# Earlier issue of the first w_in quarter, held-back loads of the next group, and a new spacing of the first stages, in a fused attention and FFN kernel

## The chip, the cores and the metric

The kernel runs on one core of one Trainium2 chip. The metric is the device time of one execution in microseconds (us), lower is better. Executions of one kernel agree within about 1% here. All times below are medians of runs whose state is "fast" (or of a single profile, where that is said). Engines: PE (matrix), PEld (its weight loads), DVE (vector), ACT (scalar), POOL (GpSimd), SP (sync, which issues most DMA transfers). The program holds one list of instructions for each engine, and the framework puts semaphore waits in where one engine needs another's result.

## The reference

Sliding-window causal attention on q, k, v of shape (8, 8, 576, 64) with a window of 64 keys, then a feed-forward block on the 4608 tokens:

```python
scores = q @ k^T / sqrt(64);  only keys with 0 <= i - j < 64 count
attn   = softmax(scores) @ v            # -> x, 4608 x 512
h      = maximum(x @ w_in, 0)           # w_in 512 x 2048
out    = (h * h) @ w_out                # w_out 2048 x 512, result float32
```

## The kernel before

The 4608 tokens are 36 chunks of 128, taken in groups of four. Per chunk `S(i)` computes scores and the masked exponentials, `V(i)` multiplies them with v, `X(i)` transposes x, and `U(i, fq)` multiplies with one quarter of w_in; `TR` transposes k and q of a group; `out_proj`, the multiplication with w_out, follows a group later. Only the first two groups (the start) matter here; from group 2 on a steady loop runs.

v is kept in eight slots, each as two tiles: `v_ev[i]` holds chunk i, and `v_od[i]` holds the same rows shifted by 64, so that its lower half is the end of the chunk before. The cast of chunk i therefore writes three tiles, the last of them in the slot of its successor:

```python
    NV = 8
    def cast_v(i, st):
        v_ev, v_od, v_next = v_evs[i % NV], v_ods[i % NV], v_ods[(i + 1) % NV]
        nc.gpsimd.tensor_copy(out=v_ev[:, :, 0:D], in_=st[:])
        nc.gpsimd.tensor_copy(out=v_od[64:P, :, 0:D], in_=v_ev[0:64, :, 0:D])
        if i + 1 < NCK:
            nc.gpsimd.tensor_copy(out=v_next[0:64, :, 0:D], in_=v_ev[64:P, :, 0:D])
    # values(i), the value matmuls, read v_ods[i % NV] and v_evs[i % NV], all 128 rows
```

The start of the program, in order of emission (cut):

```python
    nc.vector.memset(v_ods[0][0:64, :, 0:D], 0.0)
    ...                                  # casts and transposes of k, q of group 0
    for i in range(2):
        cast_v(i, vst[i])                # POOL
    for quar in range(3):
        load_w_in(quar)                  # POOL issues: float32 in HBM, float16 in SBUF
    for i in range(2, 4):
        cast_v(i, vst[i])
    kst[1], qst[1] = load_kq(k, 1), load_kq(q, 1)   # SP issues
    for i in range(4, 8):
        vst[i] = load(v, i)
    ...                                  # casts of k, q of group 1, load_w_in(3)
    warm(2), S(0), warm(2), S(1), warm(3)
    V(0), S(2), warm(2), X(0), V(1), S(3), X(1), warm(1), V(2), U(0, 0), X(2), V(3), U(1, 0)
    ...
    U(3, 2), TR("q", 1, 0, acopy)
    for i in range(4, 8):
        cast_v(i, vst[i])
        if i > 4:
            load_w_out(i - 5)
    load_w_out(3)
    U(0, 3), ...
```

The program is emitted by one Python thread. The framework works out semaphore waits from the order of emission: a read waits for the writes of the same bytes that were emitted ahead of it, and a write for the reads emitted ahead of it. `warm` is a matmul on zeros that is meant to keep the clock up.

The softmax here doesn't subtract the row's maximum and nothing guards it: scores larger than these inputs give would overflow.

## Time and profile before

| what | value | view |
|---|---|---|
| median time of the first three runs | 337.8 us | runs |
| PE busy | 92% of 337.3 us | page, part 1 |
| longest wait of PE | 7.1 us, for w_in | waits |
| mean granted clock, 20 to 40 us | 0.74 | windows |
| first matmul of group 2's `up` | 99.5 us | timeline |

From the page: the span in 40 slices of 8.4 us, each digit the busy share in tenths (PEclk: the granted clock in tenths).

```profile
PE   7728987799899999999999999999999999999994
PEclk9976997799999999999999999999999999999999
DMA  7999999942929569958989796989589021100111
```

The loss is in the first eight slices or so: PE has gaps, the clock falls, and DMA is busy all the time. After that PE is full.

Waits of PE in the first 120 us (engine, line, what for, us in total, times, longest):

```profile
PE hps L293 <- DMA w_in<-in_moe_w_in_dram: 7.1, 1, 7.1
PE xt_ps L257 <- DVE x_sb L247: 5.0, 7, 2.2
...
```

The timeline of PE (start, duration, what; in brackets the idle time before it and its releaser) shows the wait and the cold clock: the first `U`, 16 matmuls, takes 1.89 us, and 1.06 us when warm.

```profile
14.57 0.22 PE L242 MATMUL av<-v_od,pm 128*64 128x65 f16 x1
...
26.87 1.89 PE L293 MATMUL hps<-xT,w_in 128*128 128x128 f16 x16 [7.15 <-DMA w_in<-in_moe_w_in_dram]
...
44.43 1.06 PE L293 MATMUL hps<-xT,w_in 128*128 128x128 f16 x16
```

The DMA view of two windows of 1 us, from 20 and from 21 us (queue: packets, MB, share of the 16 DMA engines). q0 carries the transfers that POOL issues, q1 those of SP. w_in, issued at 14.59, moves nothing before 21.4 us:

```profile
q1 hardware_dynamic: 148, 0.15, 109.0%
...
q1 hardware_dynamic: 182, 0.19, 69.9%
q0 software_dynamic: 64, 0.07, 38.6%
```

### The profile page before, as it was taken

How to read it: one execution, taken by the hardware profiler on the slowest of the kernel's cores; microseconds unless marked ns; L12 is line 12 of the kernel's file. 1: busy time of each engine (PE TensorE's matmuls, PEld its weight loads, DVE VectorE, ACT ScalarE, POOL GpSimd, SP SyncE). 2: the span in 40 equal slices, each digit the busy share in tenths (PEclk: the TensorE clock that was granted, in tenths of full speed). 3: DMA queues.
4: the chain of work that ended last, by engine and by line, in shares of the span. 5: the costliest groups of instructions: out<-in, count | busy, mean ns of one | idle time of the engine just before them, and what ended most of it. 6: DMA issues, size and time to landing. Idle time of an engine off the chain costs nothing.

```text
span 337.3 us, 7237 instructions
## 1 busy us (share of the span) xinstructions
PE 308.7 (92%) x2891; PEld 165.8 (49%) x2891; DVE 183.5 (54%) x424; ACT 158.6 (47%) x272; POOL 113.4 (34%) x188
## 2 busy tenths in 40 slices
PE   7728987799899999999999999999999999999994
PEld 3317976578444544454444444444443444444441
DVE  3753676554666664575476557646574665334400
ACT  3612693237445554553555355545544554444311
POOL 1782682780526160535063416333451000000000
PEclk9976997799999999999999999999999999999999
DMA  7999999942929569958989796989589021100111
GB/s 248 206 221 200 221 220 198 219 86 73 180 87 194 121 134 225 211 119 191 226 154 206 151 230 123 212 171 231 119 186 216 35 62 32 63 31 33 62 62 63
DMA packets 136737, 50.79 MB, mean 151 GB/s; under 512 B 121856, under 2 KB 132096, under 8 KB 136704
## 3 DMA queue, kind: packets, MB, share of 16 engines
q1 hardware_dynamic: 132480, 46.15, 65.2%
q0 software_dynamic: 4224, 4.19, 7.3%
q8 instruction: 22, 0.36, 0.5%
q14 instruction: 11, 0.09, 0.1%
HBM read 36.70 MB, written 9.44 MB: 137 GB/s over the span
## 4 chain that ended last, share of the span: by engine, by line
PE 59%; DMA 19%; DVE 7%; ACT 6%; SPq 5%; POOL 2%; issue 2%; POOLq 0%; ACTq 0%
PE ops L310 26%; PE hps L281 19%; DMA qT<-q 7%; PE hps L293 7%; DMA st<-in_v_dram 7%; DMA w_in<-in_moe_w_in_dram 4%; PE av L242 3%; PE sc L218 3%; DVE h L275 3%; ACT hrelu L274 2%; SPq L196 2%; DVE pm L231 2%; ACT pm L227 1%; DVE x_sb L247 1%; ACT qT L191 1%
## 5 line engine op out<-in xcount | busy, mean ns | idle before, releaser
L275 DVE SCALAR_TENSOR_TENSOR h<-hps,hrelu 128x512 f16<-128x512 f32 x144 | 99.4, 690 | 119.6 <-ACT hrelu L274 119.1
L310 PE MATMUL ops<-w_out,h 128*128 128x512 f16 x576 | 146.5, 381 | 0.0
L274 ACT ACTIVATE hrelu<-hps 128x512 f32<-128x512 f32 x144 | 86.2, 599 | 116.7 <-PE hps L281 81.6
L281 PE MATMUL hps<-xT,w_in 128*128 128x512 f16 x448 | 115.1, 379 | 0.0
L310 PEld LDWEIGHTS <-h 128*128 128x128 f16 x576 | 53.8, 98 | 60.5 <-issue 0.5
L281 PEld LDWEIGHTS <-w_in 128*128 128x128 f16 x448 | 42.8, 98 | 50.1
L227 ACT ACTIVATE pm<-sc 128x512 f16<-128x512 f32 x72 | 39.0, 597 | 22.4 <-PE sc L218 21.8
L293 PE MATMUL hps<-xT,w_in 128*128 128x128 f16 x512 | 36.6, 233 | 8.4 <-DMA w_in<-in_moe_w_in_dram 7.1
L113 POOL CAST k<-st 128x512 f16<-128x512 f32 x24 | 14.9, 620 | 83.4 <-DMA st<-in_k_dram 71.9
L293 PEld LDWEIGHTS <-w_in 128*128 128x128 f16 x512 | 33.4, 105 | 11.2 <-DMA w_in<-in_moe_w_in_dram 7.3
L125 POOL CAST v_ev<-st 128x512 f16<-128x512 f32 x36 | 22.6, 629 | 35.3 <-DMA st<-in_v_dram 28.5
L316 ACT ACTIVATE osb<-ops 128x512 f32<-128x512 f32 x36 | 21.6, 599 | 22.8 <-PE ops L310 22.7
L247 DVE TENSOR_TENSOR x_sb<-av,rden 128x256 f16<-128x256 f32 x72 | 30.5, 424 | 2.5
L231 DVE TENSOR_TENSOR pm<-pm,mask_inner 128x512 f16<-128x512 f16 x56 | 26.6, 499 | 4.5 <-ACT pm L227 4.1
L126 POOL COPY v_od<-v_ev 64x512 f16<-64x512 f16 x36 | 22.5, 624 | 2.3
L128 POOL COPY v_od<-v_ev 64x512 f16<-64x512 f16 x35 | 22.2, 634 | 2.0
L242 PEld LDWEIGHTS <-pm 128*64 128x64 f16 x576 | 12.8, 113 | 15.6 <-issue 9.5
L242 PE MATMUL av<-v_od,pm 128*64 128x65 f16 x288 | 17.4, 200 | 1.7 <-DVE pm L231 1.6
L113 POOL CAST q<-st 128x512 f16<-128x512 f32 x24 | 14.8, 618 | 9.7 <-DMA st<-in_q_dram 9.7
L242 PE MATMUL av<-v_ev,pm 128*64 128x65 f16 x288 | 17.4, 201 | 0.0
L218 PE MATMUL sc<-qT,kT 64*128 64x64 f16 x504 | 15.0, 191 | 0.5 <-ACT qT L179 0.3
L218 PEld LDWEIGHTS <-kT 64*128 64x128 f16 x504 | 10.7, 95 | 4.1 <-issue 2.7
(56 smaller groups left out, 118.2 us busy)
## 6 DMA issues: line engine op xcount, KB each, us to landing
out_dram<-osb SPq DMA_DIRECT2D x36, 256.0 KB, 2.6
st<-in_v_dram SPq DMA_DIRECT2D x32, 256.0 KB, 5.8
st<-in_k_dram SPq DMA_DIRECT2D x21, 256.0 KB, 4.3
st<-in_q_dram SPq DMA_DIRECT2D x21, 256.0 KB, 4.9
w_in<-in_moe_w_in_dram POOLq DMA_DIRECT2D x4, 512.0 KB, 14.4
w_out<-in_moe_w_out_dram POOLq DMA_DIRECT2D x4, 512.0 KB, 13.0
kq_st<-in_k_dram SPq DMA_DIRECT2D x1, 1024.0 KB, 5.5
kq_st<-in_q_dram SPq DMA_DIRECT2D x1, 1024.0 KB, 8.0
```

The lines of the kernel that those rows point to most:

```text
L113: copy(out=kq16(key, i // 4)[:, :, i % 4, :].rearrange("p a (b d) -> p a b d", d=D), in_=st[:].rearrange("p (a b) d -> p a b d", b=2))
L125: nc.gpsimd.tensor_copy(out=v_ev[:, :, 0:D], in_=st[:])
L218: nc.tensor.matmul(sc[hh][:, hp, blk, :], keys, qTs["q", g][r0:r0 + 64, hp, a + 64 * blk:a + 64 * blk + 64], start=True, stop=True)
L227: nc.scalar.activation(out=pm[:], in_=sc[hh][:], func=AF.Exp, scale=1.0 / float(D) ** 0.5)
L231: nc.vector.tensor_tensor(out=pm[:], in0=pm[:], in1=mask, op=ALU.min)
L242: nc.tensor.matmul(av[64 * blk:64 * blk + 64, h % 4, 0:65], pms[i][h % 2][:, h // 2, blk, :], vv[:, h, 0:65], start=True, stop=True)
L247: nc.vector.tensor_tensor(out=x_sb[:, 2 * half:2 * half + 2, i % 2, :].rearrange("p c (b d) -> p c b d", d=D), in0=av[:, :, 0:D].rearrange ...
L274: nc.scalar.activation(out=hrelu, in_=hps, func=AF.Relu, scale=H_SCALE)
L275: nc.vector.scalar_tensor_tensor(out=out, in0=hps, scalar=0.0, in1=hrelu, op0=ALU.max, op1=ALU.mult)
L281: nc.tensor.matmul(hps[:], w_in_q[f // 4][:, c, f % 4 * P:(f % 4 + 1) * P], xT_of(g)[:, :, c, :], start=(c == 0), stop=(c == DMC - 1))
L293: nc.tensor.matmul(hps[:, f, :], w_in_q[fq][:, c, f * P:(f + 1) * P], xT_of(g)[:, i % 4 // 2, c, a:a + P], start=(c == 0), stop=(c == DMC ...
L310: nc.tensor.matmul(hold[ts % 2][:], h2s["h", g][:, 4 * fq + f, ts * P:(ts + 1) * P], w_out_q[fq][:, f, :], start=(fq == 0 and f == 0), sto ...
```

## The change

The intent: bring the first w_in quarter in earlier. It is issued behind the cast of chunk 0 instead of chunk 1; the loads of the next group are held back by a 2-byte transfer that reads the second w_in quarter, so that SP issues nothing more until that quarter has landed; the same is done with w_out and group 2. The first stages are then spaced anew, and the casts of v chunks 4 to 7 are written further up in the program. The core of the diff:

```diff
+    gate16 = const.tile([1, 8], FP16, name="gate16")
+    def behind(w, n):
+        nc.sync.dma_start(out=gate16[:, n:n + 1], in_=w[0:1, 0, 0:1])
@@ start
-    for i in range(2):
-        cast_v(i, vst[i])
-    for quar in range(3):
-        load_w_in(quar)
+    cast_v(0, vst[0])
+    load_w_in(0)
+    cast_v(1, vst[1])
+    load_w_in(1)
+    load_w_in(2)
     for i in range(2, 4):
         cast_v(i, vst[i])
+    behind(w_in_q[1], 0)
     kst[1], qst[1] = load_kq(k, 1), load_kq(q, 1)
@@ the same loop, moved up over the first S, V, X, U
+    for i in range(4, 8):
+        cast_v(i, vst[i])
+        if i > 4:
+            load_w_out(i - 5)
+    load_w_out(3)
     warm(2), S(0), warm(2), S(1), warm(3)
-    V(0), S(2), warm(2), X(0), V(1), S(3), X(1), warm(1), V(2), U(0, 0), X(2), V(3), U(1, 0)
+    V(0), S(2), warm(3), V(1), X(0), S(3), warm(2), V(2), X(1), U(0, 0), V(3), X(2), U(1, 0)
     ... (U, TR, S of group 0 and 1 reordered, six more warm matmuls)
-    for i in range(4, 8):
-        cast_v(i, vst[i])
-        if i > 4:
-            load_w_out(i - 5)
-    load_w_out(3)
+    behind(w_out_q[1], 1)
     kst[2], qst[2] = load_kq(k, 2), load_kq(q, 2)
@@ spacing of group 1: new fractions, e.g.
-        steps += [(0.01 + 0.08 * j, V, 4 + j), (0.05 + 0.08 * j, X, 4 + j)]
+        steps += [(0.02 + 0.1 * j, V, 4 + j)] if j else []
+        steps += [(0.03 + 0.115 * j, X, 4 + j)]
     ...
-                steps.append((0.88, transposes_xbar, g + 2))
+                steps.append((0.8, transposes_xbar, g + 2))
```

## The prediction

> **What bounds it.** Over the whole span PE is 92% busy, and from 140 us on it is bound by PE (58.6 of 60 us busy, windows view). The loss lies in the first 70 us, which DMA bounds: the 40 slices show DMA at 90% or more there and 2 tenths just after 70.
>
> - PE waits 7.15 us (19.6 to 26.9, timeline) for the first w_in quarter. It was issued at 14.59 and landed 12.2 us later. The DMA queues by 1 us window show no byte of the software queue before 21.3 us; until then the hardware queue moved group 1's k and q. The first w_out quarter did the same: issued at 40.2, first bytes 46.6.
> - The idle time drops the granted clock to 0.50 from 22 to 32 us; an up_chunk takes 1.9 us there, against 0.9 warm: about 2.9 us lost.
> - From 50 to 66 us come waits on x_sb and xT (2.2, 0.7, 1.6 us) and two more cold stretches (0.5 to 0.6): about 8 us in all.
>
> Total loss before 100 us: 18 to 20 us.
>
> **Why w_in is late.** The Trainium skill ("DMA: Bandwidth & Descriptors", "Queues, rings and completion order") says that an engine round-robins between queues at packet granularity. The trace agrees once both flow (about 155 packets of each per us, 27 to 34 us), not for the 6 us before. My reading: descriptors of the hardware queue already taken in (some 1,100 packets, 70 per engine) go first. Rival: a software DMA has some 6 us of latency anyway. No view separates them; I give the first 75%.
>
> **The change.** Engine orders differ only before group 2: SP gains two 2-byte transfers and keeps its order, POOL moves one w_in issue up by one cast_v (2.0 us), PE reorders and gains six warm matmuls (0.2 us each). From group 2 on all orders are equal; moving transposes_xbar from 0.88 to 0.80 passes nothing on SP, so it is worth 0.
>
> **Expected course.** First w_in issue 12.6 instead of 14.6, bytes from about 14.3 (v finishes at 13.7), a quarter takes 3.1 to 3.4 us of packets: landing about 18, before U(0,0) needs it (19.3). The 7 us wait and the cold stretch go: about 9 us ahead at U(0,1). Given back: group 1's k and q now start at about 22 instead of 13.5 and land at about 27.5 and 32; the fourth w_in, issued behind the cast of k, lands about 36, so U(0,3) waits 1 to 2 us. V(4) comes about 7 us earlier than 48.4. Then w_out flows without competition at about 40, kq of group 2 starts near 48 behind the second w_out, and the wider spacing should take some 3 to 5 us of the x_sb and cold losses. Some waits for late TR and v_8 casts come back.
>
> Sum: 9 − 2 + 4 − 1 = about 10 us, nearly all on the critical path, since all after it is PE-bound and unchanged.
>
> **Predicted:** 327.5 us (range 320.5 to 336.5). Faster by over 2%: 0.74; within 2%: 0.23; slower: 0.03.
>
> **What would show it.** Right: first software-queue bytes at 14 to 15 us; no wait of U for w_in above 1 us; granted clock 1.00 from 20 to 32 us; the first L281 matmul of group 2 near 89 instead of 99.6; equal periods (32 us) after. Wrong: bytes at about 19 (issue + 6) mean the latency theory; then w_in costs 3.5 us still and the fourth quarter lands at 44 to 46, with a wait of 5 us or more before U(0,3), and the gain shrinks to 0 to 3 us.
>
> **What would make it wrong.** That latency; kq of group 2 landing after 60 us and stalling TR; DVE (about 70% busy once the stage is squeezed) becoming the limit.

## More of the kernel before

POOL, same view: the three w_in issues, and the last copy of `cast_v(7)`, the one that writes `v_ods[0]`.

```profile
14.59 2.36 POOL L138 DMA_DIRECT2D w_in<-in_moe_w_in_dram  x3
...
44.99 0.61 POOL L128 COPY v_od<-v_ev 64x512 f16<-64x512 f16 x1
```

So `V(0)` ran at 14.57, thirty microseconds ahead of that copy.

## The result, and the profile after

| kernel | median us (runs) | ratio to before, 95% interval |
|---|---|---|
| before | 337.99 (337.05 to 339.36) | |
| changed | 360.25 (359.33 to 360.89) | 1.0653 (1.0606 to 1.0700) |

The result is correct, and 6.5% slower. All ratios in this document are the mean time of one kernel's fast runs over the mean of the other's fast runs of the same rounds, so they are not quite the ratio of the medians quoted.

The page of the changed kernel (span 357.3 us, slices of 8.9 us):

```profile
PE   8400098879999999999999999999999999999994
PEclk9955569989999999999999999999999999999999
DMA  7999899970018759695799879599967611300021
```

PE does nothing at all for three slices. The waits of PE, in a window from 10 to 115 us:

```profile
PE av L247 <- POOL v_od L129: 30.7, 1, 30.7
PE xt_ps L262 <- DVE x_sb L252: 2.7, 5, 1.7
PE hps L298 <- DVE xT L265: 1.5, 2, 1.2
...
```

The wait for w_in is gone. In its place stands one single wait of 30.7 us, of the value matmuls (L247) for a v_od copy of POOL. The timelines of PE and of POOL name both ends of it:

```profile
13.90 0.82 PE L307 MATMUL warm<-zeros 128*128 128x512 f16 x3
45.44 0.22 PE L247 MATMUL av<-v_od,pm 128*64 128x65 f16 x1 [30.72 <-POOL v_od L129]
```
```profile
12.56 0.87 POOL L139 DMA_DIRECT2D w_in<-in_moe_w_in_dram  x1
...
44.78 0.61 POOL L129 COPY v_od<-v_ev 64x512 f16<-64x512 f16 x1
```

The copy that ends at 45.39 is the last one of `cast_v(7)`; `V(0)` starts 0.05 us after it. What `V(0)` waits for is not its own v, cast by 12.6 us, but the v of chunk 7.

The DMA side did what was predicted. In the changed kernel the 1 us windows from 13 and from 14 us give:

```profile
q1 hardware_dynamic: 174, 0.04, 26.5%
...
q0 software_dynamic: 47, 0.05, 50.9%
```

The first w_in bytes move at 14.1 us, 7.3 us earlier than before. And the stages behind the stall are shorter: `V(0)` is 30.9 us later than before (45.44 against 14.57), but group 2's first `up` matmul only 20.5 us later (119.9 against 99.5), and the span 20.0 us longer. That is no sign that the cure works: e2 below has the stall but neither the early w_in nor the new spacing, and its stages are shortened as much (first value matmul at 44.96 us, group 2 at 119.9). The loads land while PE stands still (in e2 all four w_in quarters by 36.8 us). Under the stall the rest of the change is worth 1 us at most (360.25 against 361.23 us in e2), which is within the scatter.

**Theory A.** `V(0)` is now emitted behind `cast_v(7)`, which writes the lower half of `v_ods[0]`. The framework has to take this as a read after a write, and makes `V(0)` wait for chunk 7's cast. In the kernel before it was a write after a read, which POOL had long to satisfy. **Rival B:** the held-back loads make the v chunks late, and `V(0)` shows it. **Rival C:** the emission of the loop ahead of the matmuls costs as such, whatever the slot.

### The profile page after: what moved, and what is told of

Its sections match the earlier page's. It is cut to its first block, busy times and chain, and to the rows that moved or that the text cites. A ratio compares the mean times of both kernels' runs of the same rounds, so it can differ in the third digit from the quotient of the medians.

```text
span 357.3 us, 7251 instructions
## 1 busy us (share of the span) xinstructions
PE 308.1 (86%) x2897; PEld 164.7 (46%) x2897; DVE 185.1 (52%) x424; ACT 158.9 (44%) x272; POOL 113.0 (32%) x188
## 4 chain that ended last, share of the span: by engine, by line
PE 53%; DMA 20%; POOL 7%; SPq 6%; DVE 6%; ACT 5%; issue 2%; POOLq 0%; ACTq 0%
PE ops L315 23%; PE hps L286 17%; DMA st<-in_v_dram 7%; DMA qT<-q 7%; PE hps L298 6%; PE sc L223 3%; PE av L247 3%; DMA kq_st<-in_q_dram 3%; DVE h L280 3%; SPq L201 2%; ACT hrelu L279 2%; SPq L84 2%; POOL v_ev L126 2%; POOL v_od L127 2%; DMA w_in<-in_moe_w_in_dram 2%
## 5 line engine op out<-in xcount | busy, mean ns | idle before, releaser
L286 PEld LDWEIGHTS <-w_in 128*128 128x128 f16 x448 | 42.8, 98 | 50.1
L247 PE MATMUL av<-v_od,pm 128*64 128x65 f16 x288 | 17.0, 201 | 31.6 <-POOL v_od L129 30.7
L298 PE MATMUL hps<-xT,w_in 128*128 128x128 f16 x512 | 33.6, 224 | 2.0 <-DVE xT L265 1.5
L247 PEld LDWEIGHTS <-pm 128*64 128x64 f16 x576 | 12.9, 114 | 46.0 <-issue 40.2
L298 PEld LDWEIGHTS <-w_in 128*128 128x128 f16 x512 | 31.0, 100 | 4.8 <-issue 2.9
L321 ACT ACTIVATE osb<-ops 128x512 f32<-128x512 f32 x36 | 21.6, 600 | 24.4 <-PE ops L315 24.4
L251 DVE RECIPROCAL rden<-av 128x4 f32<-128x4 f32 x72 | 12.5, 173 | 30.5 <-PE av L247 30.4
L247 PE MATMUL av<-v_ev,pm 128*64 128x65 f16 x288 | 17.0, 202 | 0.0
```

What stands on the lines that cost most here:

```text
L247: nc.tensor.matmul(av[64 * blk:64 * blk + 64, h % 4, 0:65], pms[i][h % 2][:, h // 2, blk, :], vv[:, h, 0:65], start=True, stop=True)
L286: nc.tensor.matmul(hps[:], w_in_q[f // 4][:, c, f % 4 * P:(f % 4 + 1) * P], xT_of(g)[:, :, c, :], start=(c == 0), stop=(c == DMC - 1))
L298: nc.tensor.matmul(hps[:, f, :], w_in_q[fq][:, c, f * P:(f + 1) * P], xT_of(g)[:, i % 4 // 2, c, a:a + P], start=(c == 0), stop=(c == DMC ...
```

## The experiments

Ten kernels ran, one of them twice (e4 and e11); all gave correct results. "Before" ran in the same rounds on the same chip.

| run | what | us | ratio to before (95%) |
|---|---|---|---|
| e1_v0_first | changed, `V(0)` emitted ahead of the casts | 331.99 | 0.9801 (0.9761 to 0.9841) |
| e2_before_early | before, casts emitted early | 361.23 | 1.0672 (1.0637 to 1.0707) |
| e3_no_gates | changed, no held loads | 358.55 | 1.0585 (1.0546 to 1.0625) |
| e4_nine_slots | changed, nine v slots | 330.03 | 0.9745 (0.9712 to 0.9778) |
| e5_first_gate | e1, second hold removed | 330.33 | 0.9759 (0.9734 to 0.9784) |
| e6_no_gates_v0 | e1, both holds removed | 334.44 | 0.9882 (0.9855 to 0.9909) |
| e7_loads_only | before, early w_in and both holds | 336.94 | 0.9954 (0.9929 to 0.9978) |
| e8_spacing_only | e1, w_in as before, no holds | 335.00 | 0.9890 (0.9869 to 0.9911) |
| e9_nine_first_gate | e4, second hold removed | 330.50 | 0.9766 (0.9742 to 0.9789) |
| e10_fourth_early | e9, fourth w_in quarter earlier | 331.30 | 0.9796 (0.9769 to 0.9822) |
| e11_nine_again | e4 again | 330.30 | 0.9759 (0.9726 to 0.9793) |

### What makes the stall: e1 to e4

**e1_v0_first.** The edit moves `V(0)` over the loop, and with it the calls ahead of `V(0)`: the scores of chunks 0 and 1 and some warm matmuls, which had all run by 14.7 us in the changed kernel too. In the traces the instruction lists of all five engines are the same as in the changed kernel, instruction by instruction; only waits differ.

```diff
+    warm(2), S(0), warm(2), S(1), warm(3)
+    V(0)
     for i in range(4, 8):
         cast_v(i, vst[i])
         ...
-    warm(2), S(0), warm(2), S(1), warm(3)
-    V(0), S(2), warm(3), V(1), ...
+    S(2), warm(3), V(1), ...
```

> Only V(0), the value matmuls of chunk 0, is emitted ahead of the loop that casts v chunks 4 to 7; the order of instructions on each of the five engines is the same as in the changed kernel. Theory A (V(0) emitted behind cast_v(7) has to wait for it, because cast_v(7) writes the lower half of v_od slot 0, which V(0) reads): the 30.7 us wait of PE for v_od goes to under 1 us, the 357.3 us span falls to 322 to 330 us. Rival B (the held loads of group 1 make v late, so the wait stays): wait above 20 us, time within 5 us of the changed kernel's 360.

Measured 331.99 us, span 329.5, at the edge of what theory A gave for the span. The value matmuls start at 14.74 us; no wait for v_od is left among the waits of PE, whose longest in total are:

```profile
PE xt_ps L262 <- DVE x_sb L252: 2.1, 5, 1.2
PE av L247 <- DVE pm L236: 1.7, 4, 0.5
PE hps L298 <- DMA w_in<-in_moe_w_in_dram: 1.5, 1, 1.5
...
```

Rival B is refuted: the loads are held back exactly as in the changed kernel.

**e2_before_early.** The converse: the kernel before, with nothing but the loop of casts moved up. Here too all engines' lists are unchanged.

```diff
+    for i in range(4, 8):
+        cast_v(i, vst[i])
+        ...                  # w_out issues, as in the loop
     warm(2), S(0), warm(2), S(1), warm(3)
     V(0), ...
-    (the same loop, further down)
```

> The kernel before, with only the loop of casts of v chunks 4 to 7 (and w_out issues) emitted ahead of the first scores and V(0); engine orders unchanged, no held loads, old spacing. Theory A: PE waits for v_od from about 15 us until the last copy of cast_v(7), 45.6 us, some 30 us, and as the 7 us wait for w_in and 3 us of cold clock are swallowed by it, the time is 352 to 362 us. Rival B (the held loads are the cause): as before, 337 to 339 us.

Measured 361.23 us: the whole loss of the change, made by the moved loop alone, the part of it with no apparent effect. Its waits of PE:

```profile
PE av L242 <- POOL v_od L128: 30.2, 1, 30.2
...
```

`cast_v(7)` ends at 44.91 us in this run, the first value matmul starts at 44.96.

**e3_no_gates.** The changed kernel without its two `behind` lines.

> The changed kernel without the two small transfers that hold back loads. Theory A: the wait of V(0) stays, ending with cast_v(7) at 43 to 46 us, about 28 to 31 us long; time 350 to 360 us. Rival B (the held loads cause the wait): wait under 3 us, time 325 to 338 us.

Measured 358.55 us, and the stall stays:

```profile
PE av L247 <- POOL v_od L129: 29.9, 1, 29.9
...
```

**e4_nine_slots.** `NV = 8` becomes `NV = 9` in the changed kernel; the order of emission stays, and DVE gets two more memsets, for the ninth slot.

> The changed kernel with nine slots for v in place of eight, so that the lower half written by cast_v(7) lies in slot 8, not in slot 0; the order of emission stays as changed. Theory A: same cure as e1 by other means, wait for v_od under 1 us, time within 2 us of e1. Rival C (it is the place of emission itself, not the shared slot, that makes the wait): wait of 30 us stays, time 355 to 362 us.

Measured 330.03 us, first value matmul at 14.92 us, no wait for v_od:

```profile
14.92 0.22 PE L247 MATMUL av<-v_od,pm 128*64 128x65 f16 x1
...
```

Rival C is refuted: it takes the early emission and the shared slot together. Theory A has now been shown both ways, by taking away either of its two conditions and by making the stall in the kernel before. One difference stays open: e4 is 2.0 us under e1 in the same rounds (329.07 to 331.19 against 330.59 to 333.39 us), and no run tells why.

### What the rest of the change is worth: e5 to e8

These four ran in the same rounds. e5 and e6 take the `behind` lines out of e1; e7 puts the early w_in issue and both `behind` lines into the kernel before; e8 is e1 with the w_in issues of before and no `behind`. As diffs:

```diff
 e5:  -    behind(w_out_q[1], 1)
 e6:  -    behind(w_in_q[1], 0)
      -    behind(w_out_q[1], 1)
 e8, on top of e6:
      -    cast_v(0, vst[0]); load_w_in(0); cast_v(1, vst[1]); load_w_in(1); load_w_in(2)
      +    for i in range(2): cast_v(i, vst[i])
      +    for quar in range(3): load_w_in(quar)
 e7, on top of before:
      -    for i in range(2): cast_v(i, vst[i])
      -    for quar in range(3): load_w_in(quar)
      +    cast_v(0, vst[0]); load_w_in(0); cast_v(1, vst[1]); load_w_in(1); load_w_in(2)
      +    behind(w_in_q[1], 0)      # ahead of the loads of group 1
      +    behind(w_out_q[1], 1)     # ahead of the loads of group 2
```

> e1 without the second small transfer (group 2's loads are no longer held behind the second w_out quarter). Theory (a software DMA starts behind what the hardware queue has taken in): first w_out bytes 6 to 7 us after its issue instead of 1.5 us, w_out later by 5 to 8 us, so some waits for w_out; k and q of group 2 some 10 us earlier, which nothing on PE waits for. Time within 3 us of e1 (332), 330 to 336.

> e1 without both small transfers. Theory (hardware queue's 1,250 packets go first): first w_in bytes near 19.5 us as in e3, first quarter landed near 24.5 to 25 us, PE waits 3 to 5 us for w_in and its clock goes cold; time 333 to 339 us, 3 to 6 us over e1. Rival (the holding itself is worth nothing, only the early issue counts): time equal to e1 within 1 us.

> The kernel before with only the early issue of the first w_in quarter and the two small transfers; its own spacing and its own place of the casts. Theory (the loads are what pays): first w_in bytes near 14.3, the 7 us wait for w_in and the cold stretch go, time 328 to 334 us, 5 to 9 us under before. Rival (the new spacing is what pays): 336 to 340 us.

> e1 with only the new spacing: w_in issued as before behind chunk 1, no small transfers. Theory (the loads are what pays): wait for w_in 6 to 8 us as before, time 334 to 339 us. Rival (the new spacing is what pays): 329 to 333 us.

Measured, in the order e5, e6, e7, e8: 330.33, 334.44, 336.94, 335.00 us. Their waits of PE for w_in, one line of each, in the same order:

```profile
PE hps L298 <- DMA w_in<-in_moe_w_in_dram: 1.0, 1, 1.0
...
```
```profile
PE hps L298 <- DMA w_in<-in_moe_w_in_dram: 5.0, 1, 5.0
...
```
```profile
PE hps L298 <- DMA w_in<-in_moe_w_in_dram: 2.9, 1, 2.9
...
```
```profile
PE hps L298 <- DMA w_in<-in_moe_w_in_dram: 7.0, 1, 7.0
...
```

- The hold on group 1's loads is worth 4.1 us (e6 minus e5). Without it the wait for w_in is back with 5.0 us and the clock falls (0.55 from 20 to 30 us). The 333 to 339 us expected of e6 held.
- The early issue without the hold gives 0.6 us (e8 minus e6), within the scatter. The first w_in bytes then move at 19.9 us instead of 21.6: the issue is 2 us earlier, but the 7 us before the first byte stay.
- The hold on group 2's loads is worth nothing on PE's path: e5, without it, is at 330.33, e1, with it, at 331.99 on another chip, and e9 and e11, which differ in it alone and ran together, at 330.50 and 330.30. The prediction of e5 was right in mechanism (the first w_out bytes move at 48.8 us instead of 43.3) and right that little depends on it (one wait of 0.6 us for w_out).
- Neither half alone gives the gain. The loads alone (e7) are 1.7 us under before: the 7 us wait is gone, but the old spacing then waits 2.9 us for the fourth w_in quarter and 5.1 us in all for x_sb (5.0 before), and the clock stands at a mean of 0.83 from 40 to 60 us (0.91 before). What each of these costs no run separates. My expectation for e7, 328 to 334, was wrong. The spacing alone (e8) is 3.6 us under before, although its wait for w_in is a full 7.0 us; my expectation of 334 to 339 held. Together (e5, e1) they give 8.3 and 6.6 us.

### A better version: e9 to e11

e9 puts the two best edits together (nine slots, no second hold), e10 also issues the fourth w_in quarter right behind the third, e11 repeats e4 beside them.

```diff
 e9, on top of changed:  NV = 9,  and  -    behind(w_out_q[1], 1)
 e10, on top of e9:
      load_w_in(2)
 +    load_w_in(3)
      ...
 -    load_w_in(3)            # behind the casts of group 1's k
```

> The changed kernel with nine v slots and without the second small transfer: the two best single edits so far together. If they add up, 327.5 to 329.5 us; if the second transfer is worth nothing either way, equal to e11 within 1 us (329 to 331).

> e9 with the fourth w_in quarter issued right behind the third, before the casts of group 1's k, to take away the wait of U(0,3) for it (1.0 us in e5). Expected: that wait goes to 0, group 1's k and q land up to 3 us later; PE may then wait for the casts of q instead. Gain over e9 0 to 1.5 us; a loss of up to 1 us if the later k and q are what binds.

> The kernel of e4 again, beside e9 and e10 on the same chip: 329 to 331 us, 2 to 3% under before.

Measured 330.50, 331.30 and 330.30 us. e9 and e11 are equal within their intervals. e10 gained nothing: it is 0.8 us over e9, the second of the two outcomes that its expectation allowed. Its wait for the fourth quarter is indeed gone, but the transposes of q now wait 1.6 us for the casts of POOL (0.2 us in e9), and the waits for x_sb rise from 1.9 to 2.8 us:

```profile
PE run_ps L193 <- POOL q L120: 1.6, 4, 1.1
...
```

So the repaired change is 2.0 to 2.6% faster than before and beats both kernels, as e1 (eight slots), e4 or e9; for e1 the 95% interval reaches below 2%. I would keep e5's form or e9's; their difference is not measurable here.

## Why the prediction was wrong

**The step that failed** is "Engine orders differ only before group 2 ... POOL moves one w_in issue up by one cast_v", from which I went straight to times. The listing of instructions that I read compares the order on each engine, and in that respect moving the loop of casts is no change at all: POOL's list comes out nearly the same. What moved is which side of `V(0)` the write of `v_ods[0]` stands on in the order of emission, and so the value of POOL's semaphore that `V(0)` waits for. The listing marks that matmul as waiting for POOL before and after alike. The programs built from the recorded kernels show the value, which no view of the profile does: `V(0)` waits until POOL's semaphore has reached 7, set by the second copy of `cast_v(0)`, in before and in e1, and 37, set by the last copy of `cast_v(7)`, in the changed kernel and in e2. The term missing from the sum is +30.7 us of wait, of which 28.1 us reach the path (group 2 starts at 119.9 us as changed and 91.8 us in e1, with the same order on each engine).

Point by point:

- *w_in late because of what the hardware queue has taken in, 75%:* held. With the hardware queue empty by the end of the issue the first w_in bytes came 1.6 us after its start (e1, e4 and changed: 1.58, 1.60, 1.58); with group 1's loads queued it took 6.8 us (before), 6.9 (e3) and 6.6 (e2). Counted from the end of the issue, 1,247, 1,251 and 1,253 packets of the hardware queue went first, and at w_out 1,258 to 1,299 in the same three kernels. A fixed latency of 6 us, the rival, is refuted. The mechanism behind the count is not shown by any view.
- *First bytes at about 14.3, first quarter in time:* 14.14 us, and `U(0,0)` has no wait for w_in in e1. Held.
- *U(0,3) waits 1 to 2 us for the fourth quarter:* 1.5 us in e1, 0.6 in e4, 1.0 in e5. Held.
- *Second hold harmless:* held (e9 against e11).
- *transposes_xbar from 0.88 to 0.80 worth nothing:* SP's list is the same, and the busy time of PE from 140 to 200 us, 58.6 of 60 us, is the same before and after.
- *Group 2 starts near 89 us:* 90.5 to 91.8 us in e4, e5 and e1. Without the stall the course ended at 330 to 332 us (e4, e5, e1), inside the range; 327.5 was 2.5 to 4.5 us too low. The term that was too large is the first, "about 9 us ahead at U(0,1)": `U(0,1)` starts at 32.8 us before and at 26.3 in e1, 26.9 in e4 and 27.4 in e5, so 5.4 to 6.5 us ahead. The 3 to 5 us put in for the spacing agree with the 3.6 us of e8, although `U` still runs cold for a time (mean clock 0.91 from 40 to 60 us in e1, as before).
- *"Slower: 0.03":* far too small for a change that rearranges emission in a program whose waits follow from emission.

The mean clock and PE's busy time from 20 to 40 us (windows view; before, changed, e1) sum it up in one line each; the columns are window, length, busy us of PE, PEld, DVE, ACT, POOL, granted clock, DMA share, GB/s:

```profile
20.00:40.00 20.00, 12.61 (x189) 12.23 (x190) 9.11 (x21) 5.44 (x10) 9.97 (x17) 0.74 1.18 212
```
```profile
20.00:40.00 20.00, 0.00 (x0) 0.00 (x0) 0.00 (x0) 0.00 (x0) 9.77 (x18) 0.50 1.13 215
```
```profile
20.00:40.00 20.00, 16.38 (x274) 14.39 (x272) 13.14 (x28) 11.63 (x18) 8.42 (x15) 1.00 1.13 208
```

The Trainium skill ("TensorE: Matmul & The Clock Gate", Part 1) describes a busy state at full clock and an idle state at half of it; the 0.50 of the idle window and the 1.00 of the busy one agree.

Why was the result still correct? By the code (no run tests it): `V(0)` reads the lower half of `v_ods[0]`, which was meant to be zero and held the end of chunk 7 in the changed kernel, but the mask of a sequence's first block sets the probabilities of just these rows to zero. A slot whose reader comes after the wrong writer went unnoticed thanks to that, and only the time told.

## What to carry to other kernels

When a framework derives waits from the order of emission, moving a block of code can change no engine's order and still cost 30 us: for every block that moves, list what it writes, modulo the number of buffers and including writes into a neighbour's slot, and ask which readers it has passed. Compare waits with the value they wait for, not just orders. And when a transfer is wanted early, look at what is already queued ahead of it: issuing it 2 us sooner gave 0.6 us, holding back the loads that were queued gave 4.1 us.

## What the Trainium skill lacked or had wrong

- "DMA: Bandwidth & Descriptors", "Queues, rings and completion order", says that each engine round-robins between the queues at packet granularity. That fits once both flow (before, 27 to 34 us: about 155 packets of each per us), but not the start: a software-queue transfer began only after 1,247 to 1,299 packets of the hardware queue (some 80 per engine), 6.1 to 6.9 us after its issue in six cases of three kernels (before, e2, e3). With 256-byte packets ahead (fourth w_in quarter) it was 1,687 packets and 3.0 us (changed), 1,465 and 2.7 us (e1), 752 and 1.8 us (e4): no fixed time, and no fixed count either. That section has no such backlog, and the runs do not show where it sits.
- The same page, "Specifications", gives about 1 us to the first byte for a software-generated DMA. With the hardware queue idle from the end of the issue on, the runs show 1.4 to 1.6 us from the start of the issue (changed, e1, e4), 0.7 to 0.9 us of which is the issuing instruction; close to the page. Its figure for a busy queue is missing.
- "Perfetto Trace Analysis", "Optimization Strategy", tells to find the gap and the instruction that updates the semaphore. That found the 30.7 us wait at once in the changed kernel's trace. No page warns that the order of emission decides which write a read waits for; e2, with every engine's list the same as in the kernel before, is 6.7% slower by it.
